# One chunk of weights per two attention steps, the products of x with w_ch between the third group's chunks, three spectrum buffers

## The chip, the cores and the metric

The kernel runs on one core of one Trainium2 chip. The time is that of one execution on the device, in microseconds (us); "before" is the median of three runs. Engines are named as in the profile: PE multiplies matrices and PEld loads their stationary operand, DVE, ACT and POOL are the vector, scalar and GpSimd engines, SP only issues DMAs here. POOL issues all loads of q, k, v and the weights, in program order.

## What is computed

Attention over 8 batches x 8 heads, 576 positions, 64 per head, causal, with an additive decay from a cumulative sum of s. Its output x (8 x 576 x 512) goes through a spectral layer: a real FFT over the positions, of which 64 modes are kept; each mode has its own complex 512x512 matrix; then the inverse FFT, a residual, and a product with w_ch.

```python
X = np.fft.rfft(x, axis=1)
Xr, Xi = (np.real(X[:, :n_modes]), np.imag(X[:, :n_modes]))
Yr = np.einsum('bmd,mde->bme', Xr, w_r) - np.einsum('bmd,mde->bme', Xi, w_i)
Yi = np.einsum('bmd,mde->bme', Xr, w_i) + np.einsum('bmd,mde->bme', Xi, w_r)
Y[:, :n_modes] = Yr + 1j * Yi
y = np.fft.irfft(Y, n=S, axis=1)
u = x + y
return (u + np.maximum(u @ w_ch, 0.0)).astype(np.float32)
```

The mode matrices w_r and w_i are 64 x 512 x 512 float32 each, 134 MB together; q, k and v are 28 MB.

## The kernel before, in words

**Attention** runs in 32 steps n = 8g + b: group g (0 to 3) holds two heads, that is 128 of the 512 columns of x, and b is the batch. A step has two `scores` (one per head), two `av`, the transposes of the next step's q and k, and the `fft` of the step before (L450). The fft writes batch b of group g into the spectrum buffer `xs[g % 2]`.

**Modes.** When the eight batches of a group are through, the group's part of the product with the mode matrices can run. It is cut into chunks of eight modes: 8 chunks per group, numbered 0 to 31 over the four groups. A chunk needs two units of weights (real, then imaginary), each 1 MB on chip as bf16, loaded by two DMAs of 512 KB. `modes(g, c)` (L470, matmuls L478) runs 16 matmuls per chunk and adds the result into `y_acc` (L498), or for the last group hands it on as `y_sb` (L502).

**Buffers of weights.** There are 64 units. The first four lie in memory that is not in use yet; from unit 4 on they go round two rings, one of five units (`wpool`) and one of three (`wpool2`), and from unit 38 on round the ring of five alone. A unit's DMA waits until the chunk that used the buffer before has run. A load also waits for the one eight places before it in POOL's queue.

**Order.** The program order is written out by hand, and each engine works through its own in order. In step n POOL issues the q and k of steps n+3 and n+4 (odd n only), the v of step n+3, and weights up to `on_chip[n]` (L254 to L270). `mode_steps` (L249) says in which step a chunk runs: chunks 0 to 3 in step 8, then 4, 5, 6, 7 in steps 9, 10, 12, 14, then nearly one chunk per step. Attention ends after chunk 23.

**x times w_ch.** The last stage needs, for each of 18 pairs of token tiles, u and z = u @ w_ch. The part of z that comes from x alone is made early for 16 pairs ("kept" pairs): x is transposed by PE and copied by DVE, multiplied by w_ch (8 matmuls), and copied away by ACT (`keep_product`, L537). Six of these pairs are made in the last six attention steps (`first_transposed` L544, `first_product` L566, matmuls L571) and kept in `wpool2`. Nine are made by `work()` (L748) between chunks 24 to 27 of the last group, some of them inside `gather`; one is made in the middle of chunk 30.

**The last group.** Chunk c of the last group (24 to 31) is transposed (`y_transposed`, L699) and, from chunk 28 on, multiplied by w_ch at once (`y_times_wch`, L707). Chunks 24 to 27 go through `gather` (L718) in one go behind chunk 27: four blocks, each of 8 matmuls with w_ch and 8 with an identity (L729), whose results ACT and DVE copy in turn (L739, L741). The two PSUM buffers that the blocks use are also those of `modes`. Behind chunk 29 come three transposes of x (L669), a product with w_ch (L682), and a smaller gather. Chunks 30 and 31 are written out with other products between their matmuls. Then 18 pairs are finished and stored (L955 on).

Of the kernel before, what the change touches and what calls it, by code (L numbers as in the profile page):

```python
# [10 lines left out]
FP32 = mybir.dt.float32  # L11
FP16 = mybir.dt.float16
# [7 lines left out]
def kernel(  # L20
# [11 lines left out]
    nc = tc.nc  # L32
# [69 lines left out]
    x_all = gp.tile([P, NG, B, NT, P], FP16, name="x_all")  # L102
    y_acc = gp.tile([P, NCK, DM], FP32, name="y_acc")

    xs = [gp.tile([P, 2, 2, 2, 2, B, HM], BF16, name=f"xs{i}") for i in range(2)]
    xs_flat = [t.rearrange("p q k h r b m -> p (q k h r b m)") for t in xs]
    ident16h = gp.tile([P, P], FP16, name="ident16h")
    Ff_sb = gp.tile([P, NT, 3 * NM], FP16, name="Ff_sb")
# [137 lines left out]


    NW = 2
    mode_steps = {B: [0, 1, 2, 3], B + 1: [4], B + 2: [5], B + 4: [6], B + 6: [7]}  # L249
    for c in range(NCK, (NG - 1) * NCK):  # L250
        mode_steps.setdefault(B + c - (0 < c % NCK < 4), []).append(c)
    used = [NW * sum(len(cs) for t, cs in mode_steps.items() if t < n) for n in range(N + 1)]
    W0 = 2
    on_chip = []  # L254
    for n in range(N):
        w = 4 + 2 * (WA + WB + NE - 2) * (n + 1) // (B + 1) if n < B else plan + (3 if n <= 2 * B else 4)
        plan = w

        nt, ring = 0, ([], [])
        while nt < min(w // 2, len(wq)):  # L260
            i = ring_of(nt)
            if i is not None:
                depth = (WA, WB)[i]
                if len(ring[i]) >= depth and ring[i][-depth] >= used[n]:
                    break
                ring[i].append(nt)
            nt += 1
        if nt < w // 2:
            plan = 2 * nt + 1
        on_chip.append(2 * nt)  # L270


    nc.sync.dma_start(out=s_sb, in_=s.rearrange("b h t -> (b h) t"))
# [176 lines left out]
    def fft(n):  # L450
        if n < 0:
            return
        g, b = divmod(n, B)
        ps = auxpool.tile([P, 2, 3 * HM], FP32, name="ft_ps", tag="aux")
        for T in range(NT):
            nT = tails[T]
            for q_ in range(2):
                nc.tensor.matmul(  # L458
                    ps[HP * q_ : HP * q_ + HP].rearrange("p h f -> p (h f)"),
                    x_all[:nT, g, b, T, q_::2], Ff_sb[:nT, T, :],  # L460
                    start=(T == 0), stop=(T == NT - 1),
                    tile_position=(0, HP * q_), skip_group_check=True,
                )
        for h in range(2):
            for q_ in range(2):
                a = ps[HP * q_ : HP * q_ + HP, h, : 2 * HM].rearrange("p (r m) -> p r m", r=2)
                a = bass.AP(tensor=a.tensor, offset=a.offset, ap=[a.ap[0], [HM, 2]] + list(a.ap[1:]))
                nc.vector.tensor_copy(out=xs[g % 2][HP * h : HP * h + HP, q_, :, h, :, b, :], in_=a)  # L468

    def modes(g, c, meanwhile=None):  # L470


        ps = auxpool.tile([P, DM], FP32, name="yp", tag="aux")
        cols = xs[g % 2].rearrange("p q k h r b m -> p q k (h r b) m")

        def product(ri, q_, cg):
            k0 = HP if ri == 1 and c == 0 and cg == 0 else 0
            nc.tensor.matmul(  # L478
                ps[32 * cg : 32 * cg + 32, :],
                cols[k0:, q_, 1 - ri, :, c * MC // 2 + cg],  # L480
                wt[(g, c, ri)][cg // 2][k0:, 2 * (cg % 2) + q_, :],
                start=(ri == 0 and q_ == 0), stop=(ri == 1 and q_ == 1),
                tile_position=(k0, 32 * cg), skip_group_check=True,
            )

        for x in range(4):
            ri, y = divmod(x, 2)
            if meanwhile and x in meanwhile:
                meanwhile[x]()
            for z in range(4):  # L490
                if meanwhile:
                    product(ri, z // 2, 2 * y + z % 2)
                else:
                    product(ri, y, z)
        if g == 0:
            nc.vector.tensor_copy(out=y_acc[:, c, :], in_=ps)
# [27 lines left out]

    ways = dict(zip(kept, "vsgmsgsgmsgsgsgs"))

    first_pairs = [i for i in kept[1:] if pairs[i][0][1] < NF and pairs[i][0][0] <= 4][:6]
    z1s, xts1 = {}, {}

    def kept_place(i, t):  # L530

# [12 lines left out]
    def first_transposed(i, x):  # L544
        b, T = pairs[i][x]
        ps = auxpool.tile([P, DT, P], FP32, name="xt_ps", tag="aux")
        for dt in range(DT):
            nc.tensor.matmul(
                ps[:, dt, :], x_all[:, dt, b, T, :], ident16h, start=True, stop=True,
                skip_group_check=True,  # L550
            )
        xts1[i, x] = spool.tile([P, DT, P], FP16, name="xt1", tag="yt")
        nc.vector.tensor_copy(out=xts1[i, x], in_=ps)

    open_unit = {}

    def half_of(pool, name):
# [8 lines left out]
    def first_product(i, x):  # L566
        if x == 0:
            kept_place(i, half_of(wpool2, "z1"))
        ps = auxpool.tile([P, DM], FP32, name="z1_ps", tag="aux")
        for dt in range(DT):  # L570
            nc.tensor.matmul(  # L571
                ps, xts1[i, x][:, dt, :], wch_sb[:, dt, :], start=(dt == 0), stop=(dt == DT - 1)
            )
        keep_product(i, x, ps)


    def mode_products(n, half=None):
        cs = mode_steps.get(n, [])
# [3 lines left out]
    with tc.tile_pool(name="sc_psum", bufs=2, space=PSUM) as scpool, \  # L582
# [6 lines left out]
        load(loads_qk(2) + loads_v(2))  # L589
        pad_p()  # L590
        for n in range(N):
            if n in (0, 2):
                nc.vector.memset(xs_flat[n // 2].bitcast(FP32), 0.0)
            tails_due = loads_tails(n // B + 1)[n % B - 3 : n % B - 2] if 2 < n % B < 5 else []
            load((loads_qk(n + LA) if n % 2 else []) + loads_v(n + LA) + tails_due, loads_w(on_chip[n]))
            if n == N // 2 + 1:
                nc.gpsimd.dma_start(out=wch_sb, in_=moe_w_ch.rearrange("(dt p) e -> p dt e", p=P))
            cum_rows(n + 1)
            scores(n, 0)
            av(n - 1, 1)  # L600
# [12 lines left out]
            i = first_pairs[n - N + len(first_pairs)] if n >= N - len(first_pairs) else None  # L613
# [8 lines left out]
            if i is not None:  # L622
                first_product(i, 1)
        av(N - 1, 1)
        fft(N - 1)
    load(loads_w(2 * len(wq)))
# [16 lines left out]
    NLOC = 5  # L643
    old = xs_flat[0]
# [6 lines left out]
    places = [finpool.tile([P, 4 * DM], BF16, name="r_sb", tag="r", bufs=3) for i in range(2)]  # L651
    places += [finpool.tile([P, 4 * DM], BF16, name=f"z1_{i}") for i in range(NLOC)]
    places.append(old[:, 4 * DM : 8 * DM])
# [33 lines left out]
    def keep(i):  # L687
        x_times_wch(i, True)
        j = late.index(i)
        kept_place(i, places[j])  # L690
        for x in range(2):
            keep_product(i, x, zs.pop((i, x)))

# [166 lines left out]
    def z_of(i):  # L860
        return [zs[i, x] for x in range(2)]

    for c in range(NCK - 2):
        yb = modes(NG - 1, c)
        for x in range(TAKE[c] - 1):
            work()
        if c == NCK - 3:
            x_transposed(late[-1])
            x_transposed(0)
        yt = y_transposed(yb, c)  # L870
        if TAKE[c]:
            work()
        if c >= NY:
            if c == NCK - 3:
# [124 lines left out]
```

## Time and profile before

| | |
|---|---|
| median of three runs | 440.62 us (440.25 to 440.73) |
| the profiled execution | 440.91 us, its span 439.1 us, mean granted TensorE clock 0.909 |
| busy share of the span | PE 78%, DVE 57%, ACT 51%, POOL 39% |
| DMA | 93.09 MB on the chip's side, mean 212 GB/s; HBM read 163.37 MB, written 9.51 MB |
| the chain that ended last | DMA 52%, PE 25%, DVE 14% |
| POOL's loads | 512 KB each for weights, 13.2 to 13.5 us from issue to landing; 288 KB for q and k; 64 KB for v |

The page cuts the span into 40 slices of 11 us. The digits are tenths of busy time; PEclk is the clock that PE was granted, in tenths of full speed. The window view gives the same for any stretch: for each engine its busy time and number of instructions, then the granted clock, the DMA engines' busy share and GB/s. In the timeline, a number in brackets is how long the engine had been idle before the row and what ended that.

### The profile page before, as it was taken

How to read it: one execution, taken by the hardware profiler on the slowest of the kernel's cores; microseconds unless marked ns; L12 is line 12 of the kernel's file. 1: busy time of each engine (PE TensorE's matmuls, PEld its weight loads, DVE VectorE, ACT ScalarE, POOL GpSimd, SP SyncE). 2: the span in 40 equal slices, each digit the busy share in tenths (PEclk: the TensorE clock that was granted, in tenths of full speed). 3: DMA queues.
4: the chain of work that ended last, by engine and by line, in shares of the span. 5: the costliest groups of instructions: out<-in, count | busy, mean ns of one | idle time of the engine just before them, and what ended most of it. 6: DMA issues, size and time to landing. Idle time of an engine off the chain costs nothing.

```text
span 439.1 us, 10583 instructions
## 1 busy us (share of the span) xinstructions
PE 344.2 (78%) x4409; PEld 205.8 (47%) x4409; DVE 252.3 (57%) x574; ACT 226.0 (51%) x421; POOL 171.4 (39%) x257
## 2 busy tenths in 40 slices
PE   1598899899695977983938548889996986769994
PEld 1365566466463534651615225555653544433441
DVE  7667776677564545672624325666655542462795
ACT  1386888268563724760725124566661442422794
POOL 6555444344354443423434334433322221130293
PEclk9998999999987969895877866999997996999999
DMA  8999999999999999999999999999999999997498
GB/s 162 207 205 207 204 206 208 207 209 207 208 206 206 209 207 210 208 209 209 205 209 209 209 208 207 207 209 206 212 211 212 211 211 211 201 208 154 160 381 345
DMA packets 68407, 93.09 MB, mean 212 GB/s; under 512 B 25276, under 2 KB 27064, under 8 KB 68360
## 3 DMA queue, kind: packets, MB, share of 16 engines
q0 software_dynamic: 61424, 81.28, 104.9%
q1 hardware_dynamic: 6936, 11.14, 7.0%
q8 instruction: 34, 0.56, 0.5%
q14 instruction: 13, 0.11, 0.1%
HBM read 163.37 MB, written 9.51 MB: 394 GB/s over the span
## 4 chain that ended last, share of the span: by engine, by line
DMA 52%; PE 25%; DVE 14%; issue 4%; POOL 2%; ACT 2%; DVEq 0%; POOLq 0%; ACTq 0%
DMA w_sb<-in_moe_w_r_dram 24%; DMA w_sb<-in_moe_w_i_dram 16%; DMA qk<-in_k_dram 8%; PE yp L478 3%; PE z_ps L682 3%; DMA qk<-in_q_dram 3%; DVE qt L359 3%; PE sc_ps L397 3%; DVE xs L468 2%; PE av_ps L433 2%; DVE x_all L443 2%; PE sc_ps L391 2%; PE tr_ps L355 2%; PE g_ps L729 2%; DMA v<-in_v_dram 2%
## 5 line engine op out<-in xcount | busy, mean ns | idle before, releaser
L405 ACT ACTIVATE p_sb<-sc_ps,cumt_sb 128x576 f16<-128x576 f32 (+1 forms) x256 | 141.9, 635 | 22.6 <-PE sc_ps L397 22.1
L397 PE MATMUL sc_ps<-qt,kt 128*128 128x512 bf16 (+2 forms) x384 | 78.7, 318 | 6.3 <-ACT kt L359 5.6
L244 POOL DMA_DIRECT2D v<-in_v_dram x72 | 51.3, 714 | 60.3 <-DMA w_sb<-in_moe_w_r_dram 11.6
L244 POOL DMA_DIRECT2D w_sb<-in_moe_w_i_dram x62 | 38.4, 621 | 89.7 <-PE yp L478 30.3
L359 DVE COPY qt<-tr_ps 64x576 bf16<-64x576 bf16 x64 | 47.8, 746 | 42.3 <-PE tr_ps L355 42.3
L478 PE MATMUL yp<-w_sb,xs 128*32 128x512 bf16 (+1 forms) x480 | 42.7, 434 | 26.9 <-DMA w_sb<-in_moe_w_i_dram 23.4
L355 PE MATMUL tr_ps<-ident,qk 64*64 64x64 bf16 x1152 | 34.8, 206 | 32.3 <-DMA qk<-in_k_dram 15.2
L244 POOL DMA_DIRECT2D w_sb<-in_moe_w_r_dram x60 | 37.3, 623 | 53.6 <-DMA w_sb<-in_moe_w_r_dram 32.9
L397 PEld LDWEIGHTS <-kt 128*128 128x128 bf16 x384 | 39.0, 106 | 35.0 <-ACT kt L359 12.2
L391 PE MATMUL sc_ps<-negm,ident 128*128 128x256 bf16 x256 | 54.6, 299 | 0.0
L355 PEld LDWEIGHTS <-qk 64*64 64x64 bf16 x1152 | 26.8, 119 | 50.3 <-DVE kt L359 19.5
L376 ACT ACTIVATE p<-sc_ps,cumt 128x64 f16<-128x64 f32 x32 | 10.0, 313 | 74.2 <-PE sc_ps L372 74.2
L433 PE MATMUL av_ps<-v,p_sb 128*128 128x65 f16 x1024 | 44.7, 198 | 1.9 <-DVE x_all L443 0.7
L359 ACT COPY kt<-tr_ps 64x576 bf16<-64x576 bf16 x32 | 22.8, 713 | 40.8 <-DVE qt L359 40.1
L433 PEld LDWEIGHTS <-p_sb 128*128 128x128 f16 x1024 | 38.0, 100 | 9.8 <-DVE x_all L443 5.6
L468 DVE CAST xs<-ft_ps 64x128 bf16<-64x128 f32 x128 | 36.7, 287 | 6.9 <-PE ft_ps L458 5.5
L438 DVE TENSOR_REDUCE den<-av_ps 128x5 f32<-128x10 f32 x64 | 10.8, 169 | 49.9 <-PE av_ps L433 48.9
L478 PEld LDWEIGHTS <-xs 128*32 128x32 bf16 (+1 forms) x512 | 17.4, 145 | 44.7 <-DMA w_sb<-in_moe_w_i_dram 26.0
L443 DVE TENSOR_TENSOR x_all<-av_ps,rcp 128x320 f16<-128x320 f32 x64 | 31.5, 491 | 2.2
L498 DVE TENSOR_TENSOR y_acc<-yp,y_acc 128x512 f32<-128x512 f32 x16 | 11.1, 691 | 28.8 <-PE yp L478 28.0
L458 PE MATMUL ft_ps<-Ff_sb,x_all 128*64 128x192 f16 (+1 forms) x320 | 24.2, 264 | 1.0 <-DVE x_all L443 1.0
L359 DVE COPY kt<-tr_ps 64x576 bf16<-64x576 bf16 x32 | 24.4, 763 | 0.4
(110 smaller groups left out, 429.5 us busy)
## 6 DMA issues: line engine op xcount, KB each, us to landing
w_sb<-in_moe_w_r_dram POOLq DMA_DIRECT2D x60, 512.0 KB, 13.5
w_sb<-in_moe_w_i_dram POOLq DMA_DIRECT2D x55, 512.0 KB, 13.2
out_dram<-r_w SPq DMA_DIRECT2D x16, 512.0 KB
v<-in_v_dram POOLq DMA_DIRECT2D x72, 64.0 KB, 11.1
qk<-in_q_dram POOLq DMA_DIRECT2D x15, 288.0 KB, 11.9
qk<-in_k_dram POOLq DMA_DIRECT2D x15, 288.0 KB, 13.2
x_all<-in_moe_w_r_dram POOLq DMA_DIRECT2D x4, 512.0 KB, 8.8
w_sb<-in_moe_w_i_dram POOLq DMA_DIRECT2D x3, 384.0 KB, 12.7
```

Source lines behind the costliest of these rows:

```text
L244: nc.gpsimd.dma_start(out=dst, in_=src)
L355: nc.tensor.transpose(ps[rows, r, :], src[rows, r, :], ident16[rows, rows])
L359: copy(out=to[:, :, :, half * RH : half * RH + RH], in_=ps[HP * i : HP * i + HP].rearrange("d r (h p) -> d h p r", h=2),)
L391: nc.tensor.matmul(ps[:, bass.ds(w * S, W)], ident16, negm[:, bass.ts(r, W)], start=True, stop=False, skip_group_check=True,)
L397: nc.tensor.matmul(ps[:, c0 : c0 + i1 - i0], keys[:, w, r, :], qh[:, i0:i1], start=False, stop=True, skip_group_check=True,)
L405: nc.scalar.activation(out=pt[:, poff[x] : poff[x] + S - w * W], in_=ps[:, w * S : (w + 1) * S - w * W], func=ACTF.Exp, bias=cumt_sb[:, x, ...
L433: nc.tensor.matmul(ps[:, I, r : r + NCH], lhsT, rhs, start=(i == 0), stop=(i == len(todo) - 1), skip_group_check=True,)
L443: nc.vector.tensor_tensor(out=x_all[:, g, b, :, D * h : D * h + D], in0=ps[:, :, 1 : NCH], in1=rcp.unsqueeze(2).to_broadcast([P, NT, D]), ...
L458: nc.tensor.matmul(ps[HP * q_ : HP * q_ + HP].rearrange("p h f -> p (h f)"), x_all[:nT, g, b, T, q_::2], Ff_sb[:nT, T, :], start=(T == 0), ...
L468: nc.vector.tensor_copy(out=xs[g % 2][HP * h : HP * h + HP, q_, :, h, :, b, :], in_=a)
L478: nc.tensor.matmul(ps[32 * cg : 32 * cg + 32, :], cols[k0:, q_, 1 - ri, :, c * MC // 2 + cg], wt[(g, c, ri)][cg // 2][k0:, 2 * (cg % 2) + ...
L682: nc.tensor.matmul(zs[i, x], xts[i][:, x, dt, :], wch_sb[:, dt, :], start=(dt == 0), stop=(last and dt == DT - 1), skip_group_check=True,)
```

## The change

It moves work and adds no arithmetic: PE has 4409 matmuls before and after, POOL the same 239 loads. DVE has one memset more.

- Weights come at one unit per attention step (with one more in steps 8, 16 and 24), so that 37 of the 64 units are issued in attention, where it was 51. After chunk 7, chunks run in about every second step, and chunk 16 is the last in attention, where it was 23.
- A third spectrum buffer is added, since group 2's chunks 17 to 23 now run after the last group's ffts have begun: groups use buffers 0, 1, 2, 0. It is zeroed in step 4.
- `first_transposed` and `first_product` go. All 15 kept pairs but the last are made by `work()`: three each behind chunks 18 to 21, one behind 22, two behind 23 and one behind 25. None is made inside `gather` or behind chunks 24, 26 and 27.
- The kept products lie in other places: first in `wpool2`.

```diff
-    xs = [gp.tile([P, 2, 2, 2, 2, B, HM], BF16, name=f"xs{i}") for i in range(2)]
+    xs = [gp.tile([P, 2, 2, 2, 2, B, HM], BF16, name=f"xs{i}") for i in range(3)]
+    XS = (0, 1, 2, 0)
...
-    mode_steps = {B: [0, 1, 2, 3], B + 1: [4], B + 2: [5], B + 4: [6], B + 6: [7]}
-    for c in range(NCK, (NG - 1) * NCK):
-        mode_steps.setdefault(B + c - (0 < c % NCK < 4), []).append(c)
+    mode_steps = {
+        B: [0, 1, 2, 3], 9: [4], 10: [5], 12: [6], 14: [7], 16: [8], 18: [9], 19: [10], 21: [11], 23: [12],
+        25: [13], 26: [14], 28: [15], 30: [16],
+    }
...
-        w = 4 + 2 * (WA + WB + NE - 2) * (n + 1) // (B + 1) if n < B else plan + (3 if n <= 2 * B else 4)
-        plan = w
...
-        on_chip.append(2 * nt)
+        w = 3 + n if n < B else 4 + n + (n - B) // B
...
+        on_chip.append(2 * w)
...
-            if n in (0, 2):
+            if n in (0, 2, 4):
                 nc.vector.memset(xs_flat[n // 2].bitcast(FP32), 0.0)
...
-            if i is not None:
-                first_transposed(i, 0)
             transposes(n + 1, 1)
             fft(n - 1)
             av(n, 0)
-            if i is not None:
-                first_product(i, 0)
-                first_transposed(i, 1)
-            if i is not None:
-                first_product(i, 1)
...
-    late = [i for i in kept if i not in first_pairs]
+    late = list(kept)
     order_z = late[:-1]
-    TAKE = (3, 2, 3, 0, 0, 0)
+    TAKE = {18: 3, 19: 3, 20: 3, 21: 3, 22: 1, 23: 2, 25: 1}
...
+    for c in range(len(done), (NG - 1) * NCK):
+        modes(c // NCK, c % NCK)
+        for x in range(TAKE.get(c, 0)):
+            work()
     for c in range(NCK - 2):
         yb = modes(NG - 1, c)
-        for x in range(TAKE[c] - 1):
-            work()
...
         yt = y_transposed(yb, c)
-        if TAKE[c]:
+        for x in range(TAKE.get((NG - 1) * NCK + c, 0)):
             work()
...
-            gather(0, NY, (1, 3), (1, 0))
+            gather(0, NY, (), (1, 0))
```

In `gather`, the argument that becomes `()` is the tuple of blocks behind which a `work()` runs.

More of the change, by code (lines that the diff above doesn't have):

```diff
@@ L248 @@
     NW = 2
-    mode_steps = {B: [0, 1, 2, 3], B + 1: [4], B + 2: [5], B + 4: [6], B + 6: [7]}
-    for c in range(NCK, (NG - 1) * NCK):
-        mode_steps.setdefault(B + c - (0 < c % NCK < 4), []).append(c)
+    mode_steps = {
+        B: [0, 1, 2, 3], 9: [4], 10: [5], 12: [6], 14: [7], 16: [8], 18: [9], 19: [10], 21: [11], 23: [12],
+        25: [13], 26: [14], 28: [15], 30: [16],
+    }
+    done = [c for t in sorted(mode_steps) for c in mode_steps[t]]
     used = [NW * sum(len(cs) for t, cs in mode_steps.items() if t < n) for n in range(N + 1)]
@@ L255 @@
     for n in range(N):
-        w = 4 + 2 * (WA + WB + NE - 2) * (n + 1) // (B + 1) if n < B else plan + (3 if n <= 2 * B else 4)
-        plan = w
-        nt, ring = 0, ([], [])
-        while nt < min(w // 2, len(wq)):
-            i = ring_of(nt)
-            if i is not None:
[L263 to L269, printed above, removed]
-        on_chip.append(2 * nt)
+        w = 3 + n if n < B else 4 + n + (n - B) // B
+        for u in range(NE, w):
+            ring = [x for x in range(NE, u + 1) if ring_of(x) == ring_of(u)]
+            depth = (WA, WB)[ring_of(u)]
+            assert len(ring) <= depth or ring[-1 - depth] < used[n], (n, u)
+        on_chip.append(2 * w)
     nc.sync.dma_start(out=s_sb, in_=s.rearrange("b h t -> (b h) t"))
@@ L467, in fft @@
                 a = bass.AP(tensor=a.tensor, offset=a.offset, ap=[a.ap[0], [HM, 2]] + list(a.ap[1:]))
-                nc.vector.tensor_copy(out=xs[g % 2][HP * h : HP * h + HP, q_, :, h, :, b, :], in_=a)
+                nc.vector.tensor_copy(out=xs[XS[g]][HP * h : HP * h + HP, q_, :, h, :, b, :], in_=a)
     def modes(g, c, meanwhile=None):
         ps = auxpool.tile([P, DM], FP32, name="yp", tag="aux")
-        cols = xs[g % 2].rearrange("p q k h r b m -> p q k (h r b) m")
+        cols = xs[XS[g]].rearrange("p q k h r b m -> p q k (h r b) m")
         def product(ri, q_, cg):
@@ L525 @@
     ways = dict(zip(kept, "vsgmsgsgmsgsgsgs"))
-    first_pairs = [i for i in kept[1:] if pairs[i][0][1] < NF and pairs[i][0][0] <= 4][:6]
-    z1s, xts1 = {}, {}
+    z1s = {}
     def kept_place(i, t):
@@ L542, in keep_product @@
         nc.vector.tensor_tensor(out=z1s[i][:, 1, xx], in0=z, in1=z1s[i][:, 0, xx], op=ALU.subtract)
[L544 to L553, printed above, removed]
     open_unit = {}
@@ L564, in half_of @@
         return t[:, :HU]
[L566 to L574, printed above, removed]
     def mode_products(n, half=None):
@@ L612 @@
             scores(n, 1)
-            i = first_pairs[n - N + len(first_pairs)] if n >= N - len(first_pairs) else None
-            if i is not None:
-                first_transposed(i, 0)
             transposes(n + 1, 1)
@@ L618 @@
             av(n, 0)
-            if i is not None:
-                first_product(i, 0)
-                first_transposed(i, 1)
-            if i is not None:
-                first_product(i, 1)
         av(N - 1, 1)
@@ L641 @@
     upool = xt.enter_context(tc.tile_pool(name="u_psum", bufs=2, space=PSUM))
-    NLOC = 5
-    old = xs_flat[0]
+    NLOC = 3
+    old = xs_flat[1]
     xt_sb = [
@@ L649 @@
     xt_sb.append(finpool.tile([P, 2, DT, P], FP16, name="xt_x"))
-    places = [finpool.tile([P, 4 * DM], BF16, name="r_sb", tag="r", bufs=3) for i in range(2)]
+    places = [lambda: half_of(wpool2, "z1")] * (2 * WB)
+    places.append(old[:, 4 * DM : 8 * DM])
+    places += [finpool.tile([P, 4 * DM], BF16, name="r_sb", tag="r", bufs=3) for i in range(2)]
     places += [finpool.tile([P, 4 * DM], BF16, name=f"z1_{i}") for i in range(NLOC)]
-    places.append(old[:, 4 * DM : 8 * DM])
+    places += [xs_flat[2][:, i * 4 * DM : (i + 1) * 4 * DM] for i in range(2)]
     places += [y_acc[:, c : c + 2, :].rearrange("p c e -> p (c e)").bitcast(BF16) for c in (0, 2)]
@@ L689, in keep @@
         j = late.index(i)
-        kept_place(i, places[j])
+        kept_place(i, places[j]() if callable(places[j]) else places[j])
         for x in range(2):
@@ L758, in work @@
             keep(i)
-    late = [i for i in kept if i not in first_pairs]
+    late = list(kept)
+    assert len(places) == len(late)
     order_z = late[:-1]
-    TAKE = (3, 2, 3, 0, 0, 0)
+    TAKE = {18: 3, 19: 3, 20: 3, 21: 3, 22: 1, 23: 2, 25: 1}
     us, rs = {}, {}
```

## The prediction

> **What bounds the kernel now.** I read the page's slices first: they say which engine is busy when.
>
> ```profile
> PE   1598899899695977983938548889996986769994
> PEclk9998999999987969895877866999997996999999
> DMA  8999999999999999999999999999999999997498
> GB/s 162 207 205 207 204 206 208 207 209 207 208 206 206 209 207 210 208 209 209 205 209 209 209 208 207 207 209 206 212 211 212 211 211 211 201 208 154 160 381 345
> ```
>
> From slice 2 to slice 36 (to 395 us) the DMA engines are full at 205 to 212 GB/s, whatever the others do. So the time is the load stream, whose last weights land at 404.9 us, and then 34 us of finishing (439.1 - 404.9). The change alters neither bytes nor loads. It can gain only what the stream idles now, or lose by making it idle, or by making PE late at its end. Hence the second view, the timeline of PE around that end:
>
> ```profile
> 363.69 0.66 PE L478 MATMUL yp<-w_sb,xs 128*32 128x512 bf16 x8 [2.07 <-DMA w_sb<-in_moe_w_i_dram]
> 366.22 1.99 PE L729 MATMUL g_ps<-wch_sb,yt_first 128*64 128x512 f16 x8 [0.68 <-ACT yt_first L704]
> 369.60 1.98 PE L729 MATMUL g_ps<-wch_sb,yt_first 128*64 128x512 f16 x8 [0.95 <-DVE yv L739]
> ...
> 374.63 1.14 PE L729 MATMUL g_ps<-wch_sb,yt_first 128*64 128x512 f16 x8
> 377.17 1.14 PE L729 MATMUL g_ps<-wch_sb,yt_first 128*64 128x512 f16 x8 [0.99 <-DVE yv L739]
> ...
> 384.47 1.09 PE L478 MATMUL yp<-w_sb,xs 128*32 128x512 bf16 x16
> ...
> 405.22 0.65 PE L478 MATMUL yp<-w_sb,xs 128*32 128x512 bf16 x4
> ```
>
> Row 1 is chunk 27, waiting for its weights; then the gather's four blocks; chunk 28 starts at 380.48, 29 at 384.47, 30 at 394.72. Chunk 28's weights had landed at 373.6: PE is 7 us late there, 0.9 us late at chunk 29 and 0.8 at chunk 30. From 394.72 to the last mode product at 405.22 the PE rows adjoin, 10.5 us without a wait, and that product starts 0.3 us after the last landing. So **PE and the stream reach the end together**: PE has no slack there.
>
> The same eight gather matmuls take 1.99 us in the first two blocks and 1.14 in the last two. The third view, busy times in stretches, shows why:
>
> ```profile
> core 0: us, PE busy (x) PEld busy (x) DVE busy (x) ACT busy (x) POOL busy (x), PEclk, DMA share, GB/s
> 34.90:38.30 3.40, 1.84 (x44) 1.26 (x42) 2.82 (x5) 2.29 (x6) 2.04 (x4) 1.00 1.25 197
> 38.30:41.70 3.40, 3.40 (x32) 2.22 (x29) 1.74 (x7) 2.02 (x4) 2.60 (x5) 0.50 1.24 205
> ...
> 263.60:267.00 3.40, 2.87 (x32) 1.41 (x32) 1.72 (x3) 0.00 (x0) 1.27 (x3) 0.50 1.17 204
> 338.70:342.10 3.40, 2.96 (x19) 2.03 (x20) 3.18 (x5) 0.00 (x0) 1.22 (x2) 0.50 1.13 214
> 362.60:366.00 3.40, 1.05 (x12) 0.43 (x12) 0.69 (x1) 0.42 (x1) 0.61 (x1) 1.00 1.12 210
> 366.00:369.40 3.40, 2.42 (x16) 1.56 (x17) 0.55 (x1) 1.22 (x3) 1.05 (x2) 0.50 1.13 212
> 369.40:372.80 3.40, 3.20 (x25) 2.74 (x25) 1.32 (x3) 1.06 (x2) 0.17 (x1) 0.50 1.12 211
> 393.30:396.70 3.40, 1.98 (x15) 0.89 (x16) 2.08 (x4) 2.02 (x4) 0.00 (x0) 1.00 1.12 212
> ```
>
> The third number from the end is the granted clock. It changes only at steps of 3.4 us. A stretch with 1.05 or 1.84 us of PE work at full clock is followed by one at 0.50; one with 1.98 is not. At 0.50, a stretch with 2.42 or 2.87 us leaves it there; one with 2.96 or 3.20 is followed by 1.00. In the gather it was the `work()` between the blocks (371.95 to 374.6) that filled 369.4 to 372.8 and brought the clock back at 372.8.
>
> **The change part by part.**
>
> *Attention, loads.* A step carries one unit (1.05 MB) and 0.43 MB of q, k and v: 7.1 us at 208 GB/s. For steps 8 to 15: 9 units, 8 x 0.43 and 0.13 MB of tails, 13.0 MB, 62.4 us. *Attention, engines.* First score matmuls of steps 4 to 8 start at 46.42, 53.05, 59.67, 66.30, 72.93: 6.63 us a step without a chunk; with one, step 12 takes 7.43. Steps 8 to 15 in rows free of DMA waits: 11.35 + 9.15 + 7.44 + 6.63 + 7.43 + 6.63 + 7.43 + 6.63 = 62.7 us. Over steps 8 to 31 I get 181 us for both. Engines do not fall behind by more than about 1 us before the loads do, and eight loads in flight (11 us of data) cover that. So the stream stays full. Attention ends near 264 us, not 334: 27 units of 4.97 us are left then, so unit 36 lands near 404.9 - 1.4 - 134 = 269. Cost 0; without the cover every microsecond by which the engines lose is one at the end.
>
> *The memset* held step 2 to 7.87 us, 1.24 over 6.63; in step 4 the loads in flight hide it. Cost 0.
>
> *The moved products.* A `work()` in a row of them takes 2.26 us (349.24 to 351.50). Three and a chunk (1.09) make 7.9 us against 9.94 for two units: hidden by the wait for weights. At half clock about 15, 5 us late per chunk; the ring of five units holds 15 us beyond the chunk at work. Cost 0. In attention six steps get 3 us shorter, which the stream hides too. The places of the products cost the same copies. POOL's queue gets no new kind of wait: a late chunk still delays only the units behind it, through the ring.
>
> *The thinned end.* Behind chunks 24 and 26 nothing runs but a transpose, behind 25 one `work()`. So PE idles 5 to 8 us per chunk before chunk 27, which therefore starts at half clock (as 362.6 to 366.0 shows with less idling). Its weights land at 363.65 as before.
> 1. Chunk 27: eight matmuls +0.45, the transposes 0.40 more: the gather starts at 367.07 (+0.85).
> 2. Gather: without `work()`, a block at half clock is 2.42 us of PE in 3.38 (369.60 - 366.22), less than the 2.87 that brought no clock back. Four blocks: 13.52, chunk 28 at 380.59 (+0.11). What the two removed products save (about 4.5 us) the clock takes.
> 3. Chunk 28 to 29: 3.99 us before; at half clock its 1.09 + 0.40 + 0.97 of PE double: 6.45. Chunk 29 at 387.04 (+2.57).
> 4. Chunk 29: 386.5 to 389.9 is full of its matmuls, so the clock returns at 389.9. Until then 1.09 is lost: 10.25 + 1.09, chunk 30 at 398.38 (+3.66).
> 5. Chunks 30 and 31: 10.5 us, PE alone, last product at 408.88. The stream ends 4 us earlier and no longer counts.
> 6. The rest, 33.9 us from 405.22, is the same code with PE, DVE and ACT nearly full: 0.
>
> Sum: span 439.1 + 3.66 = 442.8, execution 440.91 + 3.66 = 444.6. This execution stands 0.29 above the median, so I forecast **444.3**.
>
> Against the median again, an unknown at the upper end: chunk 29's small gather leaves PE idle 1.88 us (392.84 to 394.72), moved to 396.5. The stretch 396.7 to 400.1 would hold 1.72 us of PE work, next to the 1.84 that lost the clock and the 1.98 that kept it. If lost, 3.4 us at half cost 1.7 more (446.0). I do not take it, since 0.3 us decides, but keep it as an end. At the lower end the clock returns one stretch earlier and step 4 and part of 3 go: +1 to +2.
>
> The Trainium skill, "TensorE: Matmul & The Clock Gate", section "HAM oscillation — how this bites in real kernels", asks for no PE idle gaps over about 3.4 us; that speaks against this thinning. Its section "What's actually happening" lets one busy window give the clock back. The gather has no gap over 1 us, so by that rule the clock could return near 370; the sum would then be that of rival A. The row 366.0 to 369.4, which kept the clock at half, decides for me.
>
> **Rivals.**
>
> A. *The clock returns in the gather.* For it: its blocks are only 0.45 us short of 2.87. Against: that row. Then 367.07 + 3.38 + 3 x 2.54 puts chunk 28 at 378.1, 29 on its landing at 383.6, 30 at 393.85, the last product at 404.35: 0.87 earlier. The stream agrees: 380 to 390 moved 193 GB/s where 211 is usual, 0.85 us lost because chunk 28 freed its buffers late (POOL idle 13.28 us before 382.85). Time 439.8. Nothing I see gives more.
>
> B. *The change doesn't do what it says: attention cannot keep pace.* If a two-step pair takes 0.5 us more than its 14.2 us of loads, twelve pairs lose 6 us once the loads in flight are used up: 446.6, and more if the pair takes longer. For it: the sums are equal within 1%, and loads with few ahead of them leave DMA engines idle (382 to 386). Against: steps with a chunk ran at 7.43 next to 6.63, mean 7.03.
>
> C. *Half of the forecast*: the clock returns during chunk 28: +0.5 to +2, 441.1 to 442.8.
>
> **How the numbers follow.** This kernel's runs tell 0.2% (0.88 us) from no change. Forecast with its ends, 442.8 to 446.3: 0.55. A: 0.22, of which 0.10 below 439.74. B: 0.10. C: 0.13, of which 0.03 within 0.2%. Faster 0.10; same 0.12 + 0.03 = 0.15; slower 0.55 + 0.10 + 0.10 = 0.75. The range from 440.0 to 446.4 leaves out about half of A and B, 0.2 in all.
>
> **What would show it.** Right: granted clock 0.50 from about 363 to 390; gather blocks 3.4 us apart; chunk 28 near 380.6, chunk 30 near 398; a last mode product near 409, waiting for PE and not for weights. DMA full until 404. Wrong: gather matmuls at 1.14 us; or DMA under 200 GB/s between 100 and 260 us (B); or last weights landing well before 404.

## The result, and the profile after

The changed kernel takes **444.02 us** (median of four runs, 443.18 to 445.11), beside 440.44 us for the kernel before in the same rounds: ratio 1.0082, 95% interval 1.0058 to 1.0107. It is slower by 3.6 us. The profiled execution took 443.69 us, its span 441.9 us (before 439.1), its mean granted clock 0.895 (before 0.909).

The slices of the page that answer to those shown of before:

```profile
PE   1688889899999698889799996797672626769995
PEclk9999999899999898999699996898966655598999
DMA  9999999999999999999999999999999999994498
GB/s 168 207 206 205 205 206 208 207 208 208 203 205 209 207 209 209 202 205 209 208 207 209 200 211 212 210 211 211 211 211 211 212 211 211 211 215 88 151 382 347
```

The loads still fill the DMA engines up to slice 36, so the stream did not become slower. What is new is the row PEclk: 6, 6, 6, 5, 5, 5 in slices 30 to 35 (320 to 387 us), and the small PE digits 2, 6, 2, 6 in slices 31 to 34. The last `av` of attention starts at 267.66 us, where it started at 332.39 before.

The timeline of PE at the end of the stream, in the changed kernel (L472 are the mode products, L694 the gather, L647 a product of x with w_ch):

```profile
362.29 1.08 PE L472 MATMUL yp<-w_sb,xs 128*32 128x512 bf16 x8 [3.84 <-DMA w_sb<-in_moe_w_i_dram]
365.45 1.99 PE L694 MATMUL g_ps<-wch_sb,yt_first 128*64 128x512 f16 x8 [0.68 <-ACT yt_first L669]
368.84 1.98 PE L694 MATMUL g_ps<-wch_sb,yt_first 128*64 128x512 f16 x8 [0.96 <-DVE yv L704]
372.21 1.99 PE L694 MATMUL g_ps<-wch_sb,yt_first 128*64 128x512 f16 x8 [0.95 <-DVE yv L704]
375.59 1.98 PE L694 MATMUL g_ps<-wch_sb,yt_first 128*64 128x512 f16 x8 [0.95 <-DVE yv L704]
378.96 1.93 PE L472 MATMUL yp<-w_sb,xs 128*32 128x512 bf16 x16 [0.95 <-DVE yv L704]
384.85 1.88 PE L472 MATMUL yp<-w_sb,xs 128*32 128x512 bf16 x16
...
395.90 0.66 PE L472 MATMUL yp<-w_sb,xs 128*32 128x512 bf16 x8 [1.88 <-DVE yv L704]
396.50 3.35 PE L647 MATMUL z_ps<-wch_sb,xs 128*128 128x512 f16 x8
...
408.01 0.65 PE L472 MATMUL yp<-w_sb,xs 128*32 128x512 bf16 x4
```

All four gather blocks take 1.98 or 1.99 us, where before the last two took 1.14. Chunk 28 follows at 378.96, chunk 29 at 384.85, chunk 30 at 395.90. The eight matmuls at 396.50 take 3.35 us, where the same form takes 1.90 at full clock: the clock is lost a second time. The last mode product starts at 408.01, 2.79 us later than the 405.22 of before, and without a bracket: PE was not waiting. The last weights had landed at 404.02. The span grew by 2.8 us, the same amount.

Busy times in stretches of the changed kernel, cut at the steps of the clock (PE's number comes first, the clock is third from the end):

```profile
core 0: us, PE busy (x) PEld busy (x) DVE busy (x) ACT busy (x) POOL busy (x), PEclk, DMA share, GB/s
349.00:352.41 3.41, 0.29 (x8) 0.20 (x8) 0.00 (x0) 0.00 (x0) 0.61 (x1) 1.00 1.12 211
...
369.39:372.80 3.41, 2.46 (x20) 1.93 (x18) 1.30 (x3) 1.06 (x2) 0.05 (x1) 0.50 1.11 208
...
379.63:383.04 3.41, 1.88 (x17) 0.58 (x9) 0.69 (x1) 0.59 (x1) 2.45 (x4) 0.50 1.12 213
383.04:386.46 3.42, 3.42 (x20) 0.98 (x20) 0.69 (x1) 0.00 (x0) 0.22 (x1) 0.50 1.12 210
386.46:389.87 3.41, 2.35 (x27) 1.51 (x24) 3.08 (x5) 0.45 (x1) 2.17 (x4) 0.99 1.12 213
393.28:396.70 3.42, 1.27 (x25) 0.67 (x25) 2.28 (x4) 1.76 (x4) 0.00 (x0) 1.00 1.12 211
396.70:400.11 3.41, 3.41 (x12) 1.08 (x14) 0.69 (x1) 1.29 (x3) 0.00 (x0) 0.51 1.02 204
```

From 352.4 to 386.5 us the clock stands at 0.50: 34 us. Inside the gather a stretch holds 2.46 us of PE work out of 3.41, which does not bring the clock back. Only 383.04 to 386.46 does, which chunk 28's product with w_ch (from 383.03, 1.89 us) and then chunk 29 fill to the last. The stretch from 393.28 holds 1.27 us, and the next one is at half clock.

### The profile page after: what moved, and what is told of

Read it like the earlier page. It is cut to its first block, busy times and chain, and to the rows that moved or that the text cites. A ratio compares the mean times of both kernels' runs of the same rounds, so it can differ in the third digit from the quotient of the medians.

```text
span 441.9 us, 10609 instructions
## 1 busy us (share of the span) xinstructions
PE 349.6 (79%) x4409; PEld 202.2 (46%) x4409; DVE 253.4 (57%) x575; ACT 226.1 (51%) x421; POOL 171.4 (39%) x257
## 4 chain that ended last, share of the span: by engine, by line
DMA 54%; PE 21%; DVE 16%; ACT 4%; issue 3%; POOL 1%; DVEq 0%; ACTq 0%; POOLq 0%
DMA w_sb<-in_moe_w_i_dram 30%; DMA w_sb<-in_moe_w_r_dram 17%; DMA qk<-in_q_dram 7%; PE yp L472 3%; DVE qt L353 3%; PE sc_ps L391 2%; PE av_ps L427 2%; PE g_ps L694 2%; DVE xs L462 2%; DVE kt L353 2%; DVE x_all L437 2%; PE tr_ps L349 2%; PE z_ps L647 2%; PE z_ps L740 2%; PE u_ps L770 2%
## 5 line engine op out<-in xcount | busy, mean ns | idle before, releaser
L391 PE MATMUL sc_ps<-qt,kt 128*128 128x512 bf16 (+2 forms) x384 | 74.0, 304 | 7.5 <-ACT kt L353 6.2
L472 PE MATMUL yp<-w_sb,xs 128*32 128x512 bf16 (+1 forms) x480 | 47.9, 480 | 35.0 <-DMA w_sb<-in_moe_w_i_dram 24.8
L391 PEld LDWEIGHTS <-kt 128*128 128x128 bf16 x384 | 36.3, 101 | 34.9 <-ACT kt L353 15.2
L385 PE MATMUL sc_ps<-negm,ident 128*128 128x256 bf16 x256 | 51.8, 286 | 0.2
L349 PE MATMUL tr_ps<-ident,qk 64*64 64x64 bf16 x1152 | 31.4, 199 | 20.6 <-DVE kt L353 19.2
L472 PEld LDWEIGHTS <-xs 128*32 128x32 bf16 (+1 forms) x512 | 18.0, 148 | 58.5 <-issue 26.0
L427 PEld LDWEIGHTS <-p_sb 128*128 128x128 f16 x1024 | 36.7, 99 | 12.1 <-DVE x_all L437 6.4
L349 PEld LDWEIGHTS <-qk 64*64 64x64 bf16 x1152 | 24.3, 112 | 34.7 <-DVE kt L353 26.0
L496 DVE TENSOR_TENSOR y_sb<-yp,y_acc 128x512 f16<-128x512 f32 (+1 forms) x9 | 5.6, 631 | 40.9 <-PE yp L472 40.9
L647 PE MATMUL z_ps<-wch_sb,xs 128*128 128x512 f16 x96 | 25.8, 418 | 0.0
```

Of the source, the lines that this page charges most:

```text
L349: nc.tensor.transpose(ps[rows, r, :], src[rows, r, :], ident16[rows, rows])
L385: nc.tensor.matmul(ps[:, bass.ds(w * S, W)], ident16, negm[:, bass.ts(r, W)], start=True, stop=False, skip_group_check=True,)
L391: nc.tensor.matmul(ps[:, c0 : c0 + i1 - i0], keys[:, w, r, :], qh[:, i0:i1], start=False, stop=True, skip_group_check=True,)
L427: nc.tensor.matmul(ps[:, I, r : r + NCH], lhsT, rhs, start=(i == 0), stop=(i == len(todo) - 1), skip_group_check=True,)
L472: nc.tensor.matmul(ps[32 * cg : 32 * cg + 32, :], cols[k0:, q_, 1 - ri, :, c * MC // 2 + cg], wt[(g, c, ri)][cg // 2][k0:, 2 * (cg % 2) + ...
L647: nc.tensor.matmul(zs[i, x], xts[i][:, x, dt, :], wch_sb[:, dt, :], start=(dt == 0), stop=(last and dt == DT - 1), skip_group_check=True,)
```

## The experiments

The theory to test: the loss is the clock, which thinner work behind chunks 24 to 27 and in the gather takes from PE. The rivals: attention at its own pace starves the stream (B of the prediction), or the products that were moved, the loads or the buffers cost something of their own. Eleven kernels ran, each timed in five rounds beside the kernel before (440.25 us in the rounds of the first four, 440.44 in those of the next four, 440.48 in the last). Single runs of the kernel before lie between 439.48 and 443.75 us there, so one profiled execution can stand some 3 us off its median. The ratios come with a 95% interval; they are not the quotients of the medians and can differ from them by up to 0.2%.

### Two products back in the gather

```diff
-    TAKE = {18: 3, 19: 3, 20: 3, 21: 3, 22: 1, 23: 2, 25: 1}
+    TAKE = {18: 3, 19: 3, 20: 3, 21: 3, 22: 1, 23: 1}
-            gather(0, NY, (), (1, 0))
+            gather(0, NY, (1, 3), (1, 0))
```

> The changed kernel, but two of the fifteen products of x with w_ch go back between the blocks of the large gather, as before the change (one fewer behind chunk 23 and chunk 25). Attention's pace, the third buffer and all else stay changed. Theory T (the end is late because PE reaches it at half clock, and the work between the gather's blocks is what brought the clock back): full clock by the third or fourth gather block, chunk 28 about as late as before the change, chunk 30 near 395, time 440 to 441.5. Rival R1 (attention's pace or the ring starves the load stream): no effect, 443.5 to 444.5. Rival R2 (something else in the new order, its places or its waits, delays the end): 443.5 to 445.

442.17 us, ratio 1.0038 (1.0019 to 1.0058). PE in that run:

```profile
369.18 1.99 PE L694 MATMUL g_ps<-wch_sb,yt_first 128*64 128x512 f16 x8 [0.95 <-DVE yv L704]
372.37 3.32 PE L647 MATMUL z_ps<-wch_sb,xs 128*128 128x512 f16 x8
375.62 1.14 PE L694 MATMUL g_ps<-wch_sb,yt_first 128*64 128x512 f16 x8
```

The product between the blocks, run at half clock (3.32 us), fills a stretch, and the block behind it takes 1.14 again. More work in the gather, and the kernel is 1.9 us faster in the median, which is still above the 440 to 441.5 that the theory expected. What stays in this profile is a second loss of the clock at chunk 30, and the late start of the gather. The profiled execution is one of the two slowest of ten (444.67 us, the others from 440.20): its chunk 30 starts at 395.74, hardly earlier than the 395.90 of the changed kernel. So it shows the clock come back in the gather, but not where the faster executions gain.

### The kernel before with the thin gather

```diff
-    TAKE = (3, 2, 3, 0, 0, 0)
+    TAKE = (4, 3, 3, 0, 0, 0)
-            gather(0, NY, (1, 3), (1, 0))
+            gather(0, NY, (), (1, 0))
```

> The kernel before the change, with nothing of the change but this: the two products inside the large gather are made earlier, one behind chunk 24 and one behind chunk 25. Theory T: the gather's blocks run at half clock, 3.4 us apart, chunk 28 is not earlier than before, chunks 28 and 29 are slowed, time 442.5 to 445. Rivals R1 and R2 (the cause lies in attention or in the new places and waits): no loss, or 0.5 to 0.9 us of gain since chunk 28 comes earlier, 439.6 to 440.6.

440.88 us, ratio 1.0012 (0.9998 to 1.0026), outside both expectations: the theory's loss did not come. The first two blocks take 1.14 us, the last two 1.98 (at 369.76 and 373.14); the eight matmuls behind chunk 30's first half take 3.54. So the thin gather alone does cost the clock, from its third block on, and again at chunk 30. But chunk 28 then starts at 376.51 instead of 380.48, because the two products no longer stand in front of it and because chunk 27's weights landed 1.5 us earlier in this execution (362.11 against 363.64). Gain and loss about cancel: the last mode product comes at 405.26 (405.22 before). The loss of the changed kernel needs the thin stretch ahead of the gather as well, which has the clock lost before the first block.

### Gaps filled with meaningless products

```diff
+    JUNK = {26: (12, 12), 27: (12, 12), 29: (10, 0), 30: (5, 0)}
+    JUNK_GATHER = 2
...
+        head, middle = JUNK.get(g * NCK + c, (0, 0))
+        fill(head)
```

`fill(k)` issues k products of an identity with w_ch into a PSUM tile that nobody reads: the first number ahead of a chunk's first half, the second ahead of its second half, `JUNK_GATHER` behind each gather block.

> The changed kernel with idle matmuls added that nobody reads (512 columns each, into a spare PSUM buffer): 12 before each half of chunks 26 and 27, 2 behind each gather block, 10 before chunk 29, 5 before chunk 30. PE only gets more to do. Theory T: full clock through the gather, chunk 28 near 376, chunk 30 on its landing or 1 us behind it, the last mode product 3 to 4 us earlier than in the changed kernel, time 439.7 to 441. Rivals R1 and R2: 444 or more, since work is added.

442.51 us, ratio 1.0049 (1.0037 to 1.0061), between the theory's 439.7 to 441 and the rivals' 444. In its windows the clock is what the filling was for:

```profile
core 0: us, PE busy (x) PEld busy (x) DVE busy (x) ACT busy (x) POOL busy (x), PEclk, DMA share, GB/s
349.50:362.00 12.50, 11.70 (x72) 4.83 (x71) 0.69 (x1) 0.58 (x1) 3.05 (x5) 0.98 1.12 211
362.00:374.00 12.00, 9.18 (x85) 6.82 (x84) 4.59 (x7) 3.80 (x8) 1.83 (x3) 1.00 1.12 210
374.00:387.00 13.00, 9.30 (x82) 4.68 (x81) 5.76 (x9) 2.20 (x4) 4.23 (x7) 1.00 1.12 214
387.00:397.00 10.00, 8.92 (x96) 3.98 (x95) 5.35 (x8) 3.49 (x7) 0.59 (x1) 1.00 1.13 215
```

All four blocks take 1.14 us, chunk 28 starts at 375.33, and the last mode product at 404.82 waits 0.50 us for its weights: 3.2 us are back, PE follows the stream again. Yet the span is 440.6 us, only 1.3 shorter than that of the changed kernel. From the last mode product to the end it is 35.8 us, where the other two kernels have 33.9. That was a new question. One stretch answers where: after the output stores have had all engines busy,

```profile
437.40:439.40 2.00, 0.00 (x0) 0.00 (x0) 0.00 (x0) 0.00 (x0) 0.00 (x0) 0.50 0.07 26
```

a DMA share of 0.07 is about what one engine of 16 gives that is still at it for 2 us, alone. And the list of DMA queues between 416 and 422 us of that run (packets, MB, share of 16 engines' time) has a guest:

```profile
q1 hardware_dynamic: 1027, 1.98, 85.9%
q8 instruction: 1, 0.02, 2.0%
```

One packet of 16 KB of program code took 2.0% of 16 engines for 6 us, which is 1.9 us of one engine, in the middle of the stores. These are blocks of PE's code: only PE got instructions by the filling, and of the two instruction queues only this one has more packets for it (35 where it was 34, q14 has 13 in both). 34 packets for PE's 8818 matmuls and weight loads are one in about 260. In the changed kernel the last of these packets came at 410.5 us, where the engines are mostly idle; with 142 instructions more there is one packet more, and the last comes at 417.7.

### Only the gap before chunk 30 filled

```diff
+    JUNK = {30: (5, 0)}
```

> The changed kernel with 5 idle matmuls before chunk 30 only, in the 1.88 us in which PE waits for the copies of the small gather. Theory T: it removes only the second loss of the clock (396.8 to 400.2 in the changed kernel's profile, worth about 1.5 us there); where that loss happens in a run it is saved, so 442.3 to 443.3 and less spread from run to run. Rivals: 444 or 0.5 more.

443.58 us, ratio 1.008 (1.0062 to 1.0097): above the 442.3 to 443.3 of the theory, no gain in time beyond the spread of the runs. In the profile the second loss of the clock is gone (1.90 us for the eight matmuls, last mode product at 406.63, 1.4 us earlier than in the changed kernel), and 35.5 us follow it: five products more (ten instructions) were enough for a 35th code block, at 432.5 us, where it took 1.51 us of an engine.

### Filled, with the code block moved away

```diff
     JUNK = {26: (12, 12), 27: (12, 12), 29: (10, 0), 30: (5, 0)}
+    SMALL = {18: (9, 0), 19: (9, 0), 20: (9, 0), 21: (9, 0), 22: (9, 0), 23: (9, 0)}
```

`SMALL` does the same with products of 64 columns.

> The changed kernel with the filled gaps of the run before it (meaningless products on PE ahead of chunks 26, 27, 29, 30 and in the gather), and 54 more tiny meaningless products (64 columns) ahead of chunks 18 to 23, where PE waits for weights anyway; their result is not used. Theory: the 1.9 us that the filled kernel lost behind its last mode product come from one 16 KB block of PE's code, fetched at 417.7 us for 1.89 us while the output stores keep all DMA engines full; with some 250 more PE instructions than the changed kernel has, that fetch falls at about 410 again. Then: full clock from 350 us on, last mode product at 404.8, 33.9 us after it, span 438.7, time 440.6 (440.0 to 441.2), no different from the kernel before. Rival: the filling itself, or the clock that falls at the end, costs the 1.9 us: time 442.5 again, with 35.8 us after the last mode product.

**440.38 us**, ratio 0.9989 (0.9977 to 1.0000). With 54 more products, far ahead of the stretch in question, the kernel is 2.1 us faster. Its list of DMA queues between 406 and 412 us shows the block where it was wanted (1.2% of 16 engines for 6 us), and the stores now end together:

```profile
q1 hardware_dynamic: 490, 0.64, 31.6%
q8 instruction: 1, 0.02, 1.2%
```

```profile
404.70 0.65 PE L487 MATMUL yp<-w_sb,xs 128*32 128x512 bf16 x4 [0.66 <-DMA w_sb<-in_moe_w_i_dram]
```

```profile
404.70:437.00 32.30, 27.63 (x142) 11.14 (x142) 25.49 (x28) 23.90 (x48) 17.46 (x14) 1.00 0.79 301
437.00:438.60 1.60, 0.00 (x0) 0.00 (x0) 0.00 (x0) 0.00 (x0) 0.00 (x0) 0.68 0.01 4
```

The last mode product waits 0.66 us for its weights, and 33.9 us follow it. From 349 us to there the clock was lost for one step only, at 365.9 us, and PE made that up. So with its clock held, and its code block out of the way, the changed kernel is as fast as the kernel before, with all its moved products, loads and buffers in place: the 3.6 us are the clock.

### The code block alone

```diff
+    SMALL = {18: (12, 0), 19: (12, 0), 20: (12, 0), 21: (12, 0), 22: (12, 0), 23: (12, 0)}
```

> The changed kernel with 72 tiny meaningless products (64 columns) ahead of chunks 18 to 23 alone, none later; their result is not used. 144 PE instructions more put the last 16 KB code fetch where the filled kernel had it. Theory of the code fetch: half clock and last mode product as in the changed kernel (408.0), the fetch at about 420 us for 1.3 to 1.9 us, 35.5 us instead of 33.9 after the last mode product, time 445.5 (444.5 to 446.6), ratio 1.011 to 1.014. Rival: the fetch does nothing: 444.0, ratio 1.008, 33.9 us.

444.68 us, ratio 1.0089 (1.0068 to 1.0110), at the low end of the expected range in time and below that of the ratio. The block comes at 419.5 us for 1.55 us, and 35.3 us follow the last mode product instead of 33.9. The median rose by 0.7 only, within the spread of both: in the profiled execution the second loss of the clock is missing, so its last mode product came at 406.67, not at 408.0. The tail shows the theory, the time alone does not.

All profiles together, sorted by what lies between the last mode product and the end:

| run | last code block of PE starts | wait of PE for `yv` in the tail | from last mode product to end |
|---|---|---|---|
| before; changed; thin gather; filled with code moved; the three with an early unit (below) | 407.2 to 410.9 | none | 33.8 to 33.9 |
| before filled | 412.2 | 0.28 | 34.4 |
| end as before; two products in the gather | 408.5; 411.0 | 0.82; 1.14 | 34.8; 35.1 |
| filled; gap filled; code alone | 417.7; 432.5; 419.5 | none | 35.8; 35.5; 35.3 |

### The changed kernel with the end of the kernel before

```diff
-    TAKE = {18: 3, 19: 3, 20: 3, 21: 3, 22: 1, 23: 2, 25: 1}
+    TAKE = {18: 1, 19: 1, 20: 1, 21: 1, 22: 1, 23: 1, 24: 3, 25: 2, 26: 3}
-            gather(0, NY, (), (1, 0))
+            gather(0, NY, (1, 3), (1, 0))
```

> The changed kernel with attention, chunks' steps, loads and buffers as changed, but its end as in the kernel before: 3, 2 and 3 works behind chunks 24, 25 and 26 and two in the gather, one behind each of chunks 18 to 23. Theory (all of the loss is the thinned end): gather blocks 3 and 4 at 1.14 us again, chunk 28 near 380, last mode product at 404.4 to 405.3, time 440.3 (439.4 to 441.0), ratio 0.998 to 1.001. Rival (attention at its own pace costs, or the products behind 18 to 23 do): above 442, with weights landing after 405.5 or PE late at chunk 27.

441.46 us, ratio 1.0014 (0.9997 to 1.0030), between the theory's range and the rival's. This undoes one part of the change: the thinned end. 2.6 of the 3.6 us are back; its clock is full from 340 us to the end, gather blocks at 1.14. In the profiled execution (442.55 us, one of its slowest) PE waits for weights at the last mode product, which come at 405.97. Part of that is the stream, which now ran short once:

```profile
246.00:248.00 2.00, 1.83 (x21) 1.12 (x22) 1.50 (x6) 1.29 (x3) 1.62 (x3) 1.00 1.12 149
248.00:250.00 2.00, 2.00 (x42) 1.50 (x39) 1.41 (x4) 1.66 (x4) 1.33 (x3) 1.00 1.11 190
```

149 GB/s where 208 is usual. At 242 us five of the eight loads in flight are q, k and v with 64 to 288 KB, and only three are weights with 512 KB. This is a sign of rival B.

### The kernel before, filled

```diff
+    JUNK = {27: (6, 12)}
+    SMALL = {24: (16, 16), 25: (16, 16), 26: (16, 16)}
```

> The kernel before with meaningless products that hold its clock through the gather: 6 and 12 ahead of the halves of chunk 27, and 96 tiny ones (64 columns) in chunks 24 to 26, which also put the last code fetch (228 PE instructions more) at about 410 us; their result is not used. Theory (PE's end is set by the clock, the stream's by buffers that chunk 28 frees): no half clock from 360 on, first two gather blocks at 1.14, chunk 28 at 378.7 instead of 380.5, the stream idles less at 382 to 386, last mode product 404.4 to 404.9, time 439.9 (439.4 to 440.5). Rival (the clock loss there is hidden, the stream's end does not move): 440.3, and if the added work itself delays chunk 27: 441 to 442.

441.81 us, ratio 1.0031 (1.0018 to 1.0044). A miss, of the kind that the expectation named: the added products held the clock in the gather (all blocks at 1.14) but delayed chunk 27 to 366.36, so that chunk 28 started at 381.05, no earlier than the 380.48 of before. That is not all: in the profiled execution, the slowest of its twelve (443.56 us), chunk 30 starts 0.57 us later than before and the last mode product, at 407.44, 2.22 us later. In between the clock is lost once more: the eight matmuls at 395.89 take 3.55 us, where they took 1.90. Whether the kernel before gains from a clock held without delay stays open.

### One unit of weights earlier

```diff
-        w = 3 + n if n < B else 4 + n + (n - B) // B
+        w = 3 + n if n < B else 4 + n + (n - B) // B + (n >= 27)
```

This one edit was put into three kernels. With the end of the kernel before:

> The changed kernel with the end of the kernel before (as in the run with the end as before), and one unit of weights more on the chip from step 27 on, so that the last q, k and v loads do not leave the eight loads in flight short of bytes. Theory (the stream idles 0.5 to 1.0 us at 243 to 248 us because the eight loads in flight are then mostly small, and with the end restored the stream's end sets the time): no second below 190 GB/s from 240 to 250, last landing 0.5 to 1 us earlier, time 440.7 (440.1 to 441.2) against 441.46 without the unit. Rival (that idling is made up later, or something else makes the end late): 441.5 as without it.

440.93 us, ratio 1.0004 (0.9979 to 1.0028). In its windows the shortage is gone:

```profile
246.00:248.00 2.00, 1.89 (x26) 1.18 (x24) 1.25 (x5) 1.29 (x3) 0.45 (x2) 1.00 1.22 204
```

The last landing of the profiled execution (440.50 us) is at 404.82, and the time agrees with the kernel before. Against 441.46 the 0.5 us lie inside the spread of both (439.74 to 442.76 without it, 439.97 to 444.00 with it), so the price of the shortage is not settled.

With filled gaps and moved code:

> The changed kernel with filled gaps and moved code (meaningless products as in that run, their result not used), and one unit of weights more on the chip from step 27 on. Theory: PE keeps its clock and follows the landings, so 0.5 us less idling of the stream at 245 to 248 is 0.5 us at the end: 439.9 (439.4 to 440.3) against 440.38. Rival: the stream's last 5 us are set by single DMA engines that lag, not by the sum of the bytes: 440.4 again.

440.35 us, ratio 0.9987 (0.9968 to 1.0005), against 440.38 without it. The rival of that expectation holds: the last landing did not come earlier (404.96). In the last 4 or 5 us of the stream the rate falls from above 200 GB/s to 116, 124 and 140 GB/s between 402 and 403 us and lower behind, in this run, in the one without the unit and in the kernel before alike, so there the full rate does not set the end. That single engines lag is only argued.

In the changed kernel, and nothing else:

> The changed kernel, with one unit of weights more on the chip from step 27 on and nothing else. Theory (in the changed kernel PE at half clock sets the end, the stream has 4 us to spare): no change, 444.0 (443.2 to 444.8), although the stream no longer idles at 245 to 247. Rival (attention that starves the stream is part of the loss): 443.4 or less.

443.99 us, ratio 1.0060 (1.0038 to 1.0083), against 444.02. No effect, as the theory has it: PE comes last there, and the stream has 4 us to spare.

None of the eleven beats the kernel before by more than the measurement can tell. The best two (440.35 and 440.38) are level with it.

## Why the prediction was right

By its own steps, in the profiled executions. In that of the changed kernel the weights of chunk 27 landed at 362.24, in that of before at 363.64. This 1.4 us belongs to the executions and not to the change: in the thirteen profiles that landing lies between 362.11 us (the kernel before with the thin gather) and 364.01 (the kernel before, filled), so two variants of the kernel before mark both ends. So steps 1 to 4 are compared from that landing on.

- **Step 1, chunk 27 at half clock.** Forecast 3.42 us from landing to gather, measured 3.21 (365.45 - 362.24).
- **Step 2, the gather.** Forecast 13.52 us for four blocks, measured 13.51.
- **Step 3, chunk 28 to 29.** Forecast 6.45, measured 5.89. The prediction doubled the three pieces; at half clock they took 1.93, 0.61 and 1.89 us where they had taken 1.09, 0.40 and 1.04, which is 1.90 more and not 2.46.
- **Step 4, chunk 29 to 30.** Forecast 11.34, measured 11.05. The clock was to return at 389.9 and returned at 386.5, at the first step of the clock after chunk 29 began. Everything was earlier by 1.4 us and a little, so that chunk 28's product and chunk 29 filled the step before the one forecast.
- **Step 5, chunks 30 and 31.** Forecast 10.5, measured 12.11. This is the term that was mis-sized: the second loss of the clock, which the prediction priced at 1.7 us, placed at its upper end and did not take, happened. It was put down to 0.3 us on one side of a bound. But what a step of the clock holds depends on where the steps fall, and the bound itself is not sharp (below). The profiles of the changed kernel, of the thin gather, of the two products in the gather and of the kernel before filled have this loss; those of the kernel before, of the two kernels with its end, with code alone and of the changed kernel with the early unit do not (in the last the clock came back at 392.7 only). That would fit the spread of 1.9 us among the runs of the changed kernel; it is not shown for them.
- **Step 6, the rest.** Forecast 33.9, measured 33.9. It held for the change, but it is not a constant: a few more instructions make it 35.5.
- **Costs of 0.** The moved products cost nothing but the clock: with the clock held and all of them in their new places the kernel is level with before (440.38). The memset made step 4 take 7.72 us instead of 6.63 (first score matmul to first score matmul), and the stream moved 207 GB/s there. Attention cost nothing either in the changed kernel, but not for the reason given, that the stream stays full: it moved 191 and 172 GB/s in the two stretches from 244 to 248 us, where 210 is usual, which is 0.5 us lost; PE was later still.

The forecast of the median, 444.3, is 0.3 us from the 444.02 measured. In the profiles the sum was +3.66, measured +2.79: 1.4 of earlier landing and 1.07 less in steps 1 to 4, against 1.6 of the second loss. So the mechanism, steps 1 and 2 and the path to the end came as forecast, but that the total is so near is in part luck: a loss that was left out makes up for landings and steps that came earlier than forecast.

**The bounds of the clock.** The prediction took from eight rows how much PE work in a step loses the clock or brings it back. A ninth, of the same profile of the kernel before, does not obey:

```profile
335.30:338.70 3.40, 3.39 (x18) 0.93 (x19) 1.04 (x3) 0.00 (x0) 1.22 (x2) 0.50 1.11 208
```

PE was busy for 3.39 us, and the next step (338.70 to 342.10, in the prediction) was still at 0.50. At full clock, the kernel with the end as before kept it behind a step with 1.54 us (391.00 to 394.41), and the thin gather lost it behind one with 2.43 (332.22 to 335.63). Over all steps of the thirteen profiles, the best bound for losing the clock is 1.88 us and has 20 of some 1280 steps on its wrong side; the best one for its return is 2.97 us and has 12 of 344. So the sum of PE's work is a good guide, and 0.3 us on one side of a bound tells little.

**Rival A** (the clock returns in the gather) fell: 1.98 or 1.99 us in all four blocks. The rule that stood behind it, from the Trainium skill, "TensorE: Matmul & The Clock Gate", section "HAM oscillation — how this bites in real kernels", asks for no PE idle gap over about 3.4 us. No bracket inside the gather is over 0.96 us, and the clock stayed at 0.50 through all of it; and at 396.8 us it was lost behind a gap of 1.88. Here the measurement decides against the rule as a test for this kernel: gaps below 3.4 us did not keep the clock, nor did gaps below 1 us bring it back. What counted in most steps, as far as the windows show, is the sum of PE's work, not the longest gap; 2.46 us in 3.41 did not bring the clock back, 3.42 did. **Rival B** fell as the cause: the early unit takes its shortage away (205 and 203 GB/s from 244 to 248 us) and leaves 443.99. **Rival C** (the clock returns during chunk 28) fell too: the clock returned at 386.5, when chunk 29 was running.

## What to carry to other kernels

PE work that lies in the wait for data is not free to move away: it can be what holds the clock for the chain that follows, so before thinning such a stretch, add up PE's busy time per step of the clock, also for the stretch ahead of it. In these traces a 3.4-us step with less than about 1.9 us of PE work mostly lost the clock, and one with about 3 us mostly brought it back. Two products put back into the gather, 2.26 us of PE each at full clock, made the changed kernel 1.9 us faster in the median. And when a kernel gets a few instructions more, look at what the end of the program does, not only at the place of the edit.

## What the runs showed that was not expected

- **Program code shares the DMA engines.** A 16 KB block of PE's code, one in about 260 instructions of PE, took 0.9 to 1.9 us of one engine. In the stretch where the output stores keep all engines busy (some 400 GB/s from 420 to 437 us) it set the end: the tail grew by 1.6 us with ten instructions more, by 1.9 with 142 and by 1.4 with 144, and not at all with 250, which left the block at 408.0.
- **A small store waits at times.** In two profiles (end as before, two products in the gather) PE waited 0.82 and 1.14 us for `yv<-y_sb` in the tail, in others not at all. A code block ran within 2 us of its issue there, but also in profiles without the wait. The cause stays open; it may be part of the spread of those kernels.
